# One transformer block on one core: k and v of every batch loaded as nine-token runs and multiplied in four quarters of the array, more transposes done by transfers, a new hand-written order

## The chip, the cores and the metric

The kernel runs on one core of a Trainium2 chip. The metric is device time in microseconds (us), the median of several executions; lower is better. The core has five engines with a queue each: TensorE (PE in the profile, with its weight loads as PEld), VectorE (DVE), ScalarE (ACT), GpSimd (POOL) and SyncE (SP). SP and POOL issue the transfers, and 16 DMA engines carry them out.

## What is computed

Eight batches, eight heads, 576 tokens, 64 channels a head. Linear attention without a softmax, normalised per token and head, is followed by a phase-mixing layer over tokens and a channel layer:

```python
kv  = einsum('bhsd,bhse->bhde', k, v)
out = einsum('bhsd,bhde->bhse', q, kv)
x   = out / sqrt(mean(out*out, -1) + 1e-6) * g_norm      # then heads side by side: (8, 576, 512)
theta = x @ w_theta
y   = w_tok_r @ (x*cos(theta)) + w_tok_i @ (x*sin(theta))  # over the 576 tokens
u   = x + y
result = u + maximum(u @ w_ch, 0)                          # float32, (8, 576, 512)
```

## The kernel before

**Tiling.** A batch is worked on in five token tiles: four full ones of 128 tokens (j = 0 to 3) and one with the last 64 tokens, folded so that two halves of the 512 channels lie side by side. The steps of a batch are: `kv` (PE, fp32, L285; batch 0 L278), copies of kv into the block-diagonal weights `kbd` (ACT L307, DVE L309), q turned so that channels lie on partitions (batches 0 and 1 by PE transposes L302, later ones by SP transfers L330), `raw` = q times kv (PE L344, L353), squares (ACT L366), sums (DVE L375), the power -1/2 on POOL (`rt`, L382; batch 0 by ACT L387 and DVE L392), `x` (DVE L405, L414), x turned into `xT` and scaled (PE transposes named `xps`, L302, then ACT L257 or DVE L259), `th` = theta (PE L464, L467), the argument reduction (ACT L480, DVE L486, L494), sine and cosine (ACT L502, L509), `zm`, `zt` (DVE L531, L520; POOL moves of the tail L537), `y` over tokens (PE L554), `u` in `wn` (DVE L569), u turned back (PE `ups`, L302, L581), `v` (PE L464, L467), the end (DVE L617, L612) and the stores (SP L625, L629).

**Loads of k and v.** For batch 0, `pairs_in` (L191) puts two heads on 128 partitions, each partition holding nine consecutive tokens, 2304 B in one piece; it is called three times for k and three times for v. For the other batches `heads_in` (L199) fetches the first 512 tokens with four tokens a partition, 1024 B in one piece, 1024 pieces a load, and `tails_in` (L205) the last 64 tokens in 512 pieces of 256 B. The half of the tile that the tail leaves empty is set to zero by `pad` (L246).

**kv on the array.** Each fp32 product is two matmul records. In batches 1 to 7 (L285) two heads go together: both contract over 128 partitions, one writes PSUM partitions 0 to 63, the other 64 to 127; four pairs of heads by five tiles by two heads by two records make 80 records. In batch 0 (L278) the two heads of a pair lie on partitions 0 to 63 and 64 to 127, and write the PSUM half of the same number: nine tokens by two heads by two records, 36 for each of four pairs. One PSUM bank of the pool `acc` (four banks, shared by kv, th, y and v) holds a batch's kv.

**Transposes by transfer.** `x_turn_dma` (L425 on) turns x on the SP queue for batches from XD = 5 on, `u_turn_dma` (L594 on) turns u for the batches in UD = (5, 6); in the other batches PE does it through PSUM.

**Order.** Every step is a task; `TURNS` (L29) is one long list of task numbers, and `play` (L84) issues the tasks in just that order, so each engine's queue is fixed by hand. A letter behind a number puts a copy on ACT or DVE; `r15` stands for 15 filler matmuls (`idle`, L649). An engine runs its queue strictly in turn, so a row that waits holds all behind it.

Of the kernel before, what the change touches and what calls it, by code (L numbers as in the profile page):

```python
# [9 lines left out]
FP32 = mybir.dt.float32  # L10
# [19 lines left out]
0 1 8 4 5 6 7 2 18 3 9 10 11 14 15 r15 31 39 32 47 13 16 17 24 25 33 40 34A 48 23 19 20 35 49 41 36  # L30
55 50 42 51 37 52 38A 12 56D 53 54 21 63 71 57 64D 43 72 58 73 65 74 44 r2 137 133 59 45 75 46 60 66
76 138A 134A 61 62 67 77 68 79 89 125 90D 69 70 126 80 91 107 92 108 81D 78 93 98 82 116 117D 94 99
83 95 118 100 129 127 84 85 119 96 86 101 128 87 130 102 120 97 121 88 109 139 141 171 159 122 110
104 123 140 142A 103 124 111 112 105 28 29 26 22 206 27 207 208 30 201 163 135 131 202 113 136 114
106 132D 115 203 204 155 172 160 161 229 173 164 165 156 215 216 162 174 230 166 167 157 147 148 143
168 169 144 158 170 222 145 185 209 210 211 212 149 151 213 186 223D 214 146 150 152 217 231 236 153
243 218 232 237 244 219 154 220 233 205 388 366 377 187 190 175 234 357 188 221 177 192 224 191 176
178 235 225 250 226 251D 238 259 358 227 239 260D 240 193 353 354 514 355 194 356 189 195 252 180
261 196 253 181 262 228 254 245 360 361 241 255 242 263 264 268 362 363 246 256 257 265 266 364 365
247 269D 258 248 359 249 270 286 277 389 271 390 287D 278 288 182 267 391 272 273 183 279 315 367  # L40
289 274 392 275 290 393 291 276 378 311 280 292 293 281 282 379 283 323 312 319 320 430 316 324 284
368 431 294 501 525 502 536 503 504 179 285 369 317 313 318 314 380 505 370 381 321 307 308 325 303
322 326 371 304 305 309 299 300 432 310 382 403 394 433 306 404D 395D 342 301 372 383 396 373 384
397 302 374 434 435 405 347 197 508 509 510 511 406 348 436 437 385 398 407 399 408 438 198 375 386
441 440 439 506 442 295 296 344 400 343 401 513 512 409 376 387 345 402 412 515 526 297 421 422D 298
413 516 410 414 337 423 332 339 349 517 411 415 338 527 416 417 350 528 418 424 419 507 518 529 653
519 425 426 340 530 656 657 658 659 451 542 520 427 428 660 521 420 661D 522 334 537 459 452 662 523
429 543 538 333 335 524 460 453 471 472 473 551 454 539 540 531 461 455 532 552 474 673 684 346 649
650 184 651 652 533 541 456 467 457 468 469 663 534 462 458 535 470 578 327 553 664 328 554 665 579D
463 674 464 560 666 654 465 580 675 555 561D 466 676 556 557 581 558 667 582 677 562 544 563 583 564  # L50
565 685 447 448 329 490 569 545 584 686 566 567 570 585 491 443 449 444 445 546 559 678 687 450 586
446 330 688 571 690 492 668 689 547 691 572 548 669 341 821 810 336 475 679 477 726 573 568 574 727D
670 493 655 589 590 587 588 801 671 797 331 798 832 799 800 494 804 476 575 680 478 681 699 805 806
807 497 728 495 700 549 809 550 808D 496 576 729 682 701 485 692 498 672 730 577 731 480 599 600 591
811 592 593 702 481 486 683 703 822 717 607 601 812 693 705 704 694 594 602 813 814 732 733 823 696
608 603 609 604 605 595 718D 610 734 815 606 824 719 596 597 708 619 735 825 738 802 720 709 706 598
721 695 707 620 615 616 710 621 611 833 826 711 834 697 612 613 623 617 622 722 835 618 836 736 803
737 837 712 698 713 614 625 628 487 816 827 482 714 624 828 817 715 488 626 829 818 483 716 950 629
723 724 838 479 956 872 943 951 952 953 643 767 819 725 847 644 955 820 954D 763 751 764 752 768 769
765 747 748 830 749 638 957 753 831 766 770 873D 754 750 958 839 959 962 848 630 755 960 484 967 855  # L60
489 627 978 944 849 963 756 757 874 850 851 964 631 840 945 946 875 852 639 841 758 961 876 965 947
739 743 740 744 741 968 745 759 842 877 966 742 856 969 853 878 746 970 864D 879 760 640 973 771 761
# [3 lines left out]
898 899 985 904 908 983 896 993D 977 986 889 890 1096 987 900 988 1097 994 891 885 1098 892 909 1107  # L66
1099 995 1108 1018 1001 632 989 996 1109 1110 786 886 913 887 914 888 1100 997 990 1019 998 991 999
1002 1010D 782 915 910 911 1101 1020 783 916 912 1111 992 352 775 1117 637 199 1003 1118 793 937
1102 1021 1022 1023 784 1011 1004 1024 1103 1005 794 499 780 642 1123 917 796 785 648 1104 1025 1012
1119 918 928 923 1026 1013 1120 1006 1014 1105 1007 787 919 1008 924 929 1000 1132D 788 1015 1030  # L70
# [4 lines left out]
1141D 1139 1150 1142 940 1161 1162 935 1151 1152 1074 1163 1143 1164 1084 1144 1085 1069 1075 1146  # L75
# [27 lines left out]
def kernel(  # L103
# [12 lines left out]
    nc = tc.nc  # L116
    B, H, S, D = q.shape
    C = H * D
    P = 128
# [21 lines left out]
    NX, NXE = 7, 4  # L141
    QD = 2

    XD = 5
    UD = (5, 6)

    ZD = 2
# [750 lines left out]
```

## Time and profile before

| | |
|---|---|
| median of 3 runs | 220.95 us (219.73 to 222.49) |
| the profiled execution | 222.68 us, span 220.9 us |
| mean granted TensorE clock in it | 0.973 |
| DMA packets | 70059, of them 39570 under 512 B |
| bytes | 33.06 MB read from HBM, 9.44 MB written |

The profiled execution is 1.73 us above the median, and its time lies 1.8 us above its span. The busy times of an engine are sums over very different stages, so the table of stretches in the prediction is the one to read: a start that waits for loads, a middle in which several engines take turns, and a long last part.

### The profile page before, as it was taken

The page shows a single profiled execution, that of the slowest core. Times are in us where ns is not written, and L with a number is a line of the kernel's source. Part 1 is how long each engine was busy: PE and PEld are TensorE (multiplying, and loading weights), DVE is VectorE, ACT ScalarE, POOL GpSimd, SP SyncE. Part 2 cuts the span into 40 slices and gives each one's busy share as a digit, 9 for nine tenths or more (in the row PEclk, how much of TensorE's full clock was granted, in tenths as well). Part 3 has the DMA queues.
Part 4 walks back from the last instruction along what each step waited for, and adds up shares of the span by engine and source line. Part 5 has one row for each costly group of instructions (what it writes and reads, how often), then busy time and mean ns, then how long its engine had stood idle before and what let it go on. Part 6 is the DMA issues. An engine that isn't in the chain of part 4 may idle for free.

```text
span 220.9 us, 5506 instructions
## 1 busy us (share of the span) xinstructions
PE 200.5 (91%) x2177; PEld 137.7 (62%) x2177; DVE 175.2 (79%) x371; ACT 132.2 (60%) x268; POOL 97.3 (44%) x102
## 2 busy tenths in 40 slices
PE   7398699799799999989999999999999999999991
PEld 2275356596465768757578776866587746756850
DVE  4018649627989989897999988999997999999662
ACT  2028479317499249762788854947865888557050
POOL 8225930002953529556649158435724545204000
PEclk9969769999999999999999999999999999999998
DMA  6999999954999999959999976998980776764374
GB/s 229 274 275 238 236 231 234 271 163 27 260 140 209 297 183 306 122 85 258 307 203 289 137 226 137 240 240 225 163 141 12 225 181 166 178 114 117 110 262 154
DMA packets 70059, 43.43 MB, mean 197 GB/s; under 512 B 39570, under 2 KB 63762, under 8 KB 70034
## 3 DMA queue, kind: packets, MB, share of 16 engines
q1 hardware_dynamic: 55602, 35.73, 64.7%
q0 software_dynamic: 14432, 7.36, 25.0%
q8 instruction: 17, 0.28, 0.5%
q14 instruction: 8, 0.07, 0.1%
HBM read 33.06 MB, written 9.44 MB: 192 GB/s over the span
## 4 chain that ended last, share of the span: by engine, by line
PE 60%; DVE 14%; DMA 9%; POOL 8%; ACT 5%; issue 2%; POOLq 0%; DVEq 0%; ACTq 0%
PE y L554 26%; PE v L464 10%; PE th L464 10%; DMA wth<-in_moe_w_theta_dram 9%; POOL rt L382 5%; PE kv L285 5%; DVE arg L486 2%; DVE ss L375 2%; PE ups L302 2%; PE raw L344 2%; DVE x L405 2%; DVE zm L531 2%; PE th L467 2%; PE xps L302 1%; PE v L467 1%
## 5 line engine op out<-in xcount | busy, mean ns | idle before, releaser
L382 POOL TENSOR_TENSOR rt<-ss,mhalf 128x8 f32<-128x8 f32 (+1 forms) x35 | 54.9, 1572 | 81.7 <-DVE ss L375 81.5
L554 PE MATMUL y<-wT,zm 128*128 128x256 f16 (+1 forms) x512 | 76.0, 286 | 1.9 <-DVE zm L531 1.0
L554 PEld LDWEIGHTS <-zm 128*128 128x128 f16 x512 | 47.7, 98 | 17.2 <-DVE zm L531 2.6
L569 DVE SCALAR_TENSOR_TENSOR wn<-y,gcol,xT 128x256 f16<-128x256 f32 (+2 forms) x72 | 32.6, 478 | 8.2 <-PE y L554 7.7
L464 PE MATMUL th<-wth,xT 128*128 128x512 f16 x128 | 34.2, 395 | 2.0 <-DMA wth<-in_moe_w_theta_dram 1.6
L480 ACT ACTIVATE pt<-th 128x512 f32<-128x512 f32 (+1 forms) x40 | 21.8, 550 | 20.7 <-PE th L464 13.1
L464 PE MATMUL v<-wch,wn 128*128 128x512 f16 x128 | 31.6, 379 | 0.0
L486 DVE SCALAR_TENSOR_TENSOR arg<-pt,th 128x512 f32<-128x512 f32 (+1 forms) x40 | 24.8, 627 | 4.2 <-ACT pt L480 4.0
L509 ACT ACTIVATE sc<-arg,quarter 128x512 f16<-128x512 f32 (+1 forms) x40 | 27.0, 675 | 1.2 <-DVE arg L494 1.1
L502 ACT ACTIVATE sc<-arg 128x512 f16<-128x512 f32 (+1 forms) x40 | 23.4, 587 | 6.9 <-DVE arg L486 6.6
L366 ACT ACTIVATE sqb<-raw 128x512 f32<-128x512 f32 x32 | 18.5, 592 | 14.7 <-PE raw L344 13.4
L405 DVE TENSOR_TENSOR x<-raw,rt 128x512 f16<-128x512 f32 x32 | 21.8, 684 | 3.0 <-POOL rt L382 2.6
L375 DVE TENSOR_REDUCE ss<-sqb 128x8 f32<-128x520 f32 x32 | 21.8, 686 | 2.5 <-ACT sqb L366 2.3
L531 DVE TENSOR_TENSOR zm<-x,sc 128x1024 f16<-128x1024 f16 x32 | 21.7, 682 | 0.5 <-ACT sc L509 0.5
L617 DVE SCALAR_TENSOR_TENSOR us<-v,us 128x512 f32<-128x512 f32 (+1 forms) x32 | 19.4, 616 | 2.0 <-PE v L467 0.8
L307 ACT CAST kbd<-kv 64x256 f16<-64x256 f32 (+1 forms) x28 | 9.4, 334 | 19.1 <-PE kv L278 12.4
L464 PEld LDWEIGHTS <-xT 128*128 128x128 f16 x128 | 11.6, 100 | 13.4 <-issue 3.3
L588 ACT ACTIVATE us<-ups 128x512 f32<-128x512 f16 (+1 forms) x32 | 17.0, 541 | 4.1 <-PE ups L302 2.6
L537 POOL DMA_DIRECT2D zt<-zf x24 | 13.6, 574 | 12.4 <-PE v L467 11.1
L464 PEld LDWEIGHTS <-wn 128*128 128x128 f16 x128 | 11.8, 98 | 11.2 <-issue 0.6
L285 PE MATMUL kv<-vt,kt 128*64 128x64 f32 x560 | 18.3, 223 | 0.0
L554 PE MATMUL y<-wT,zt 128*128 128x320 f16 (+1 forms) x64 | 18.3, 286 | 0.0
(78 smaller groups left out, 249.2 us busy)
## 6 DMA issues: line engine op xcount, KB each, us to landing
kt<-in_k_dram SPq DMA_DIRECT2D x7, 1024.0 KB, 9.1
vt<-in_v_dram SPq DMA_DIRECT2D x7, 1024.0 KB, 8.0
out_dram<-us SPq DMA_DIRECT2D x24, 256.0 KB, 3.4
qh<-in_q_dram POOLq DMA_DIRECT2D x7, 512.0 KB, 11.3
out_dram<-vs SPq DMA_DIRECT2D x8, 256.0 KB, 2.3
zm<-in_moe_w_ch_dram SPq DMA_DIRECT2D x1, 1024.0 KB, 12.0
out_dram<-us SPq DMA_DIRECT2D x16, 64.0 KB, 2.1
kt<-in_k_dram SPq DMA_DIRECT2D x7, 128.0 KB, 7.4
```

What stands on the lines that cost most here:

```text
L285: nc.tensor.matmul(t[i * D:(i + 1) * D, hp - lo, :], kt[b % NKV][:, 2 * hp + i, j, :], vt[b % NKV][:, 2 * hp + i, j, :], start=(j == 0), s ...
L375: nc.vector.reduce_sum(out=ss[:], in_=sq_sb.pop((b, j))[:], axis=AXX)
L382: nc.gpsimd.tensor_tensor(out=rt[:], in0=ss[:], in1=mhalf[:, 0:h], op=ALU.pow)
L405: nc.vector.tensor_tensor(out=x_pair[b, p][:, :, a * HC:(a + 1) * HC].rearrange("p t (h e) -> p h t e", e=D), in0=r[:].rearrange("p (h t e ...
L464: nc.tensor.matmul(t[:], lhs(kc), w[:, kc, :], start=first, stop=last)
L480: nc.scalar.activation(out=pt[:], in_=th_ps[b, j][:], func=AFT.Copy, bias=MAGIC)
L486: nc.vector.scalar_tensor_tensor(out=arg[:, 0, :], in0=pt_sb.pop((b, j))[:], scalar=MAGIC, in1=th_ps.pop((b, j))[:], op0=ALU.subtract, op1 ...
L502: nc.scalar.activation(out=sc[:, 0, :], in_=arg_sb[b, j][:, 0, :], func=AFT.Sin, bias=0.0, scale=-TURN * SHRINK,)
L509: nc.scalar.activation(out=sc_sb[b, j][:, 1, :], in_=arg_sb.pop((b, j))[:, 1, :], func=AFT.Sin, bias=quarter[:], scale=-TURN * SHRINK,)
L531: nc.vector.tensor_tensor(out=dst, in0=x.unsqueeze(1).broadcast_to((P, 2, w)), in1=sc[:], op=ALU.mult)
L554: nc.tensor.matmul(t[:, 0:hi - lo], s, wT[:, w, lo:hi], start=n == 0, stop=n == len(z) - 1)
L569: nc.vector.scalar_tensor_tensor(out=dst, in0=y_in, scalar=gcol[:, 0:1], in1=x_in, op0=ALU.mult, op1=ALU.add,)
```

## The change

1. **Loads.** All batches load k and v with `pairs_in`: one transfer of 512 pieces of 2304 B for k and one for v, where there were four transfers of together 3072 pieces. `heads_in`, `tails_in` and `pad` are gone. Batch 0 comes in two parts instead of three.
2. **kv.** `kv_quad` works on four heads at a time. Each contracts over 64 partitions (r = 0, 1) and writes one half of the PSUM partitions (c = 0, 1), so the four products of a token lie in four different 64x64 quarters of the array. The two row halves write different PSUM banks, so a batch takes two `acc` banks. A batch has 9 tokens x 8 heads x 2 records = 144 records. `kv_out` copies each bank in halves: eight copies of 64x128 a batch where there were four of 64x256 (batch 0: sixteen of 64x64 where there were eight of 64x128).
3. **Transfers for transposes.** XD goes from 5 to 3 and UD from (5, 6) to (4, 5, 6): the x of batches 3 and 4 and the u of batch 4 are turned on the SP queue, which is ten more transfers (four of 128x8x128, two of 128x2x128, four of 128x4x128), and 36 + 16 PE transposes fewer.
4. **Order.** `TURNS` is written anew. There are 20 filler matmuls instead of 17. Of the nine copies of the token weights `wT`, six lie on DVE and three on ACT; before it was the other way round.

```diff
-0 1 8 4 5 6 7 2 18 3 9 10 11 14 15 r15 31 39 32 47 13 16 17 24 25 33 40 34A 48 23 19 20 35 49 41 36
+0 1 7 8 9 10 13 14 12 15 16 20 r11 27 5 6 3 4 19 2 r4 45 37 30D 31 28D 29 46A 38A 17 18 47 r2 53 61
...
-    XD = 5
-    UD = (5, 6)
+    XD = 3
+    UD = (4, 5, 6)
...
-    kt = [const.tile([P, H, NT, D], FP32, name=f"kt{i}") for i in range(NKV)]
+    kt = [const.tile([P, NHP, S], FP32, name=f"kt{i}") for i in range(NKV)]
...
+    def kv_quad(b, g, banks):
+        if banks is None:
+            banks = [ps.tile([P, NG, D], FP32, tag="acc", bufs=4, name="kv") for r in range(2)]
+        for j in range(NN):
+            js = slice(j * D, (j + 1) * D)
+            for c in range(2):
+                for r in range(2):
+                    at = slice(r * D, (r + 1) * D)
                     nc.tensor.matmul(
+                        banks[r][c * D:(c + 1) * D, g, :], kt[b % NKV][at, 2 * g + c, js],
+                        vt[b % NKV][at, 2 * g + c, js], start=(j == 0), stop=(j == NN - 1),
                     )
...
+    def kv_out(b, gs, r, i, eng):
+        at = slice(i * D, (i + 1) * D)
+        lo, n = gs[0], len(gs)
+        for c in range(2):
+            src = kv_ps[b, lo, r][c * D:(c + 1) * D, lo:lo + n, :]
+            h = 2 * c + r
+            dst = kbd[b % 2][at, :, at].rearrange("p (g k) e -> p g k e", k=4)[:, lo:lo + n, h, :]
+            copy_out(eng, dst, src)
...
-        pads = [add("pad", "POOL", lambda: pad(nc.gpsimd, 0), old)] if b == NKV else []
-        k_ = [add(f"load k{b}", "SP", lambda: heads_in(nc.sync, kt[b % NKV], k, b, all8), old),
-              add(f"load k{b}e", "SP", lambda: tails_in(nc.sync, kt[b % NKV], k, b, all8), old),
-              add(f"load v{b}", "SP", lambda: heads_in(nc.sync, vt[b % NKV], v, b, all8), old),
-              add(f"load v{b}e", "SP", lambda: tails_in(nc.sync, vt[b % NKV], v, b, all8), old)]
+        k_ = [add(f"load k{b}n", "SP", lambda: pairs_in(nc.sync, kt[b % NKV], k, b, 0, NHP), old),
+              add(f"load v{b}n", "SP", lambda: pairs_in(nc.sync, vt[b % NKV], v, b, 0, NHP), old)]
...
-        pad(nc.vector, 1)
```

What the new list does is seen at three places. In the rows below a name is the tile written, then what it is made of; a number is the buffer.

The first place is the start of the SP queue. Before, k and v of batch 0 come in six loads, then a tiny transfer (`gate_s`) that waits until the first v is there, the channel weights (`zm_77<-in_moe_w_ch_dram`), and then batch 1 in pieces of four tokens:

```order
L193 DMA kt_64<-in_k_dram 128x576
L193 DMA vt_66<-in_v_dram 128x576
L238 DMA gcol<-in_g_norm_dram 64x1
L244 DMA gate_s<-vt_66 1x1
L235 DMA zm_77<-in_moe_w_ch_dram 128x4x512
L200 DMA kt_65<-in_k_dram 128x8x256
L206 DMA kt_65<-in_k_dram 64x8x64
L200 DMA vt_67<-in_v_dram 128x8x256
L206 DMA vt_67<-in_v_dram 64x8x64
```

Now:

```order
L190 DMA kt_64<-in_k_dram 128x2x576
L190 DMA vt_66<-in_v_dram 128x2x576
L223 DMA gcol<-in_g_norm_dram 64x1 x2
L220 DMA zm_77<-in_moe_w_ch_dram 128x4x512
L229 DMA gate_s<-vt_66 1x1
L190 DMA kt_65<-in_k_dram 128x4x576
L190 DMA vt_67<-in_v_dram 128x4x576
L190 DMA kt_64<-in_k_dram 128x4x576
```

The channel weights have moved ahead of the waiting transfer, and batch 1 is two loads instead of four. The POOL queue beside it begins as before (q of batch 0, `w_tok_i`, `w_theta`, `w_tok_r`).

The second place is the DVE queue where batch 0 ends and batch 1 begins. `wn_85` is u of batch 0, `kbd_75` the kv weights of batch 1, `ss` the sums of batch 1. Before:

```order
L569 SCALAR_TENSOR_TENSOR wn_85<-y,gcol,xT_82 128x320
L309 COPY qT<-qps 128x512
L309 CAST kbd_75<-kv 64x4x64 x2
L569 SCALAR_TENSOR_TENSOR wn_85<-y,gcol,xT_82 128x256 x2
L375 TENSOR_REDUCE ss<-sqb_96 128x8
L569 SCALAR_TENSOR_TENSOR wn_85<-y,gcol,xT_82 128x256
```

Now:

```order
L548 SCALAR_TENSOR_TENSOR wn_85<-y,gcol,xT_82 128x320 x4
L288 CAST kbd_75<-kv 64x2x64 x2
L288 COPY qT<-qps 128x256
L288 CAST kbd_75<-kv 64x2x64 x2
L288 COPY qT<-qps 128x512
L354 TENSOR_REDUCE ss<-sqb_96 128x8
L288 COPY qT<-qps 128x512
L548 SCALAR_TENSOR_TENSOR wn_85<-y,gcol,xT_82 128x256
```

The kv copies and the first sums of batch 1 now stand ahead of the last three rows of u of batch 0. On PE the kv of batch 1 correspondingly stands after 15 of the 24 parts of y of batch 0 (a part is three matmuls), where it stood after 20.

The third place is the POOL queue of batch 1: `rt` are the powers, the DMA rows the loads of a later q. Before:

```order
L382 TENSOR_TENSOR rt<-ss,mhalf 128x8 x2
L212 DMA qh_68<-in_q_dram 128x8x256
L218 DMA qe_71<-in_q_dram 64x4x64
L382 TENSOR_TENSOR rt<-ss,mhalf 128x8 x2
L382 TENSOR_TENSOR rt<-ss,mhalf 128x4
```

Now:

```order
L197 DMA qh_68<-in_q_dram 128x8x256
L203 DMA qe_71<-in_q_dram 64x4x64 x2
L240 TENSOR_SCALAR wch<-zm_77 128x512
L361 TENSOR_TENSOR rt<-ss,mhalf 128x8 x4
L361 TENSOR_TENSOR rt<-ss,mhalf 128x4
```

The load of q that stood between the powers of batch 1 has moved ahead of all of them.

More of the change, by code (lines that the diff above doesn't have):

```diff
@@ L35 @@
[L35 to L39, printed above, removed]
@@ L155 @@
     HALVES = ((0, 2 * P), (2 * P, S))
[L156 to L157 removed]
+    kt = [const.tile([P, NHP, S], FP32, name=f"kt{i}") for i in range(NKV)]
+    vt = [const.tile([P, NHP, S], FP32, name=f"vt{i}") for i in range(NKV)]
     qh = [const.tile([P, H, NJ * D], FP16, name=f"qh{i}") for i in range(NB)]
@@ L717 @@
         ko = {}
[L718 to L726 removed]
+        first = None
+        for g in range(NG):
+            own = b == 0 or not g
+            t = add(f"kq {b} {g}", "PE",
+                    lambda b=b, g=g: kv_quad(b, g, [kv_ps[b, 0, r] for r in range(2)] if g and b else None),
+                    [*k_got[b, g], None if own else first], [PS_ACC, PS_ACC] if own else [])
+            if own:
+                first = t
+            last["kv", b] = t
+            if b and not g:
+                continue
+            gs = [g] if b == 0 else [0, 1]
+            outs = [add(f"ko{len(gs)} {b} {g}{r}{i}", "DVE" if i else "ACT",
+                        lambda e, b=b, gs=gs, r=r, i=i: kv_out(b, gs, r, i, e),
+                        [t, *of("raw", b - 2)], alt=("ACT", "DVE")) for r in range(2) for i in range(2)]
             first.readers = outs
[L728 to L730 removed]
+            ko.update({x: outs for x in gs})
         ko[2] = ko[0] + ko[1]
```

135 lines of the change are left out of this document (35 added, 100 removed), and 37 rows, old and new, of the table TURNS.

## The prediction

> **What bounds the kernel now.** I read the page's first table, then the busy times by stretch, then the chain of waits in order of time, then the groups and the timeline of the engines that the chain names.
>
> ```profile
> PE 200.5 (91%) x2177; PEld 137.7 (62%) x2177; DVE 175.2 (79%) x371; ACT 132.2 (60%) x268; POOL 97.3 (44%) x102
> ```
>
> ```profile
> core 0: us, PE busy (x) PEld busy (x) DVE busy (x) ACT busy (x) POOL busy (x), PEclk, DMA share, GB/s
> 27.80:40.60 12.80, 11.01 (x81) 6.76 (x80) 8.84 (x20) 11.23 (x21) 1.48 (x3) 0.85 1.29 238
> 40.60:52.00 11.40, 10.75 (x157) 8.70 (x155) 4.87 (x10) 2.40 (x5) 0.00 (x0) 1.00 0.68 165
> 52.00:110.00 58.00, 53.63 (x660) 36.94 (x657) 52.73 (x106) 38.15 (x78) 34.27 (x29) 1.00 1.04 207
> 110.00:210.00 100.00, 99.96 (x1015) 69.73 (x1009) 92.56 (x196) 67.38 (x134) 45.09 (x46) 1.00 0.80 173
> 210.00:221.00 11.00, 6.09 (x50) 3.27 (x48) 4.55 (x9) 3.15 (x6) 0.00 (x0) 0.93 0.58 203
> ```
>
> ```profile
> 5.42 20.46 DMA wth<-in_moe_w_theta_dram
> 25.92 1.86 PE th L464 x4
> ...
> 47.56 2.51 PE kv L285 x80
> ...
> 51.80 0.36 PE raw L344 x3
> ...
> 55.31 1.64 POOL rt L382
> 56.95 0.93 POOL qh L212
> 57.88 0.65 POOL qe L218
> 58.53 3.50 POOL rt L382 x2
> ...
> 125.68 2.86 PE y L554 x24
> ```
>
> The reader is to see four stages. Until 25.92 us the chain is one transfer, `w_theta`, and the first th. From 27.8 to 40.6 us ACT is the fullest engine (11.23 of 12.8 us). From 40.6 to 52 us PE works on y alone while DVE and ACT mostly stand (4.87 and 2.40 of 11.4 us), since the norm of batch 1 waits for its kv; then the chain runs through raw, three powers and a load issue on POOL. From 52 to 110 us PE and DVE are both about 92% busy, and PE is without work for 58.00 - 53.63 = 4.4 us. From 110 to 210 us PE has no gap at all: there, and only there, a microsecond of PE work removed is a microsecond of time, as long as DVE (92.6%) keeps up. The tail of 11 us is the same work in both kernels.
>
> **The change, part by part.**
>
> ```profile
> 16.46 1.26 PE L278 MATMUL kv<-vt,kt 64*64 64x64 f32 x36
> ...
> 133.52 0.32 PE L353 MATMUL raw<-kbd,qD 128*64 128x64 f16 x8
> ...
> 138.62 2.55 PE L285 MATMUL kv<-vt,kt 128*64 128x64 f32 x80
> 141.00 0.28 PE L581 MATMUL ups<-ident,wn 128*64 128x128 f16 x4
> ...
> 145.31 0.39 PE L302 MATMUL ups<-ident,wn 128*128 128x128 f16 x4
> 145.53 0.39 PE L344 MATMUL raw<-kbd,qD 128*128 128x128 f16 x4
> ```
>
> ```profile
> L285 PE MATMUL kv<-vt,kt 128*64 128x64 f32 x560 | 18.3, 223 | 0.0
> ...
> L353 PE MATMUL raw<-kbd,qD 128*64 128x64 f16 x48 | 1.9, 200 | 0.1
> ```
>
> *PE transposes.* Four cost 145.53 - 145.31 = 0.22 us, 0.055 each. Fifty-two go (36 of x, 16 of u), all in batches 3 and 4, by the order from the kv of batch 4 on and most of them in the stretch in which PE has no gap: -2.9 us.
>
> *kv in quarters.* A batch costs 141.00 - 138.62 = 2.38 us for 80 records. A record lasts 0.22 us and they start every (2.55 - 0.22)/79 = 0.030 us; batch 0, whose two heads use two of the four quarters, keeps the same pace (36 records in 1.26 us). So two run side by side, and a round of two takes 0.059 us. The new batch has 144 records. If four run side by side at the pace of two, it takes 36 rounds, 2.1 us: -0.24 us a batch, -1.7 us in batches 1 to 7. If still only two do, it takes 72 rounds, 4.25 us: +1.9 us a batch, +13 us in all. No row shows four at once. I take the first end: the quarters that differ in their column half already overlap (L285), quarters that differ in both do too (L278), and the four read the same partitions in the same number of streams as L285; all that is new is two row halves that write one PSUM half, into different banks. In batch 0 the 2.4 us so saved lie in the wait for loads and are worth nothing.
>
> A page speaks against this. The Trainium skill, TensorE: Matmul & The Clock Gate, Part 1, states that start-to-start never falls below about 25 ns however small a matmul is. By that rule 144 records would take 3.6 us, +1.2 a batch, +8.5 us over seven batches. The trace does not agree with it for matmuls that lie in different column halves: the eight of L353 last 0.20 us each and end within 0.32 us, so they start (0.32 - 0.20)/7 = 0.017 us apart.
>
> *Loads at the start.*
>
> ```profile
> q1 hardware_dynamic: 314, 0.65, 65.1%
> ...
> q0 software_dynamic: 981, 1.61, 78.8%
> ...
> q0 software_dynamic: 637, 0.81, 75.4%
> q1 hardware_dynamic: 633, 0.65, 38.6%
> ...
> q1 hardware_dynamic: 1625, 0.40, 111.8%
> ```
>
> ```profile
> 28.32 1.26 ACT L257 ACTIVATE xT<-xps,gcol 128x512 f16<-128x512 f16 x2
> ```
>
> ```profile
> L307 ACT COPY wT<-wps 128x576 f16<-128x576 f16 x6 | 3.6, 634 | 0.2 <-PE wps L643 0.2
> ```
>
> The queue rows are of 6 to 9, 15 to 26, 18 to 24 (two) and 54 to 57 us. From 18 to 24 us SP's queue (q1) and POOL's (q0) move 633 and 637 packets: they take turns one for one. SP's packets are of 1024 B then, and take 38.6% of 16 x 6 us over 633, 58 ns each; the 2304 B packets of 6 to 9 us take 65.1% of 16 x 3 us over 314, 99 ns. In the new kernel the packets of 2304 B also stand beside `w_theta`, which is behind some 900 of the 981 POOL packets that go from 15 to 26 us: 900 x 41 ns / 16 = 2.3 us later, so it lands at about 28 us. What hides this is ACT: by the new order the two scalings of x at 28.32 us (1.26 us) come before the landing, and two of the four copies of `wT` in that stretch (0.6 us each) go to DVE, which has 4 us free there. ACT's 11.23 us shrink by 2.5 to 8.8. It starts 2.3 us later and is through at the same 40.6 us. I cost the start at nothing; without that cover it is +2.3 us. That the channel weights pass the waiting `gate_s` changes nothing, as they stay behind the loads of batch 0 on their queue.
>
> *Loads later.* A load of 1024 + 512 pieces takes (1024 x 58 + 512 x 33)/16 = 4.8 us of the 16 engines (256 B: 111.8% of 16 x 3 us over 1625 is 33 ns), one of 512 x 99 ns takes 3.2. Fourteen loads save 22 us; four big x transposes at 1024 x 33/16 = 2.1, two small at 0.5 and four of u at 1.06 add 13.7. The transfer engines have more room than before, and no load on the chain after 30 us gets later.
>
> *Batch 1 earlier.* Its raw now stands behind 18 parts of y instead of 23 (kv after 15, three more before raw). A part is 3 x 2.86/24 = 0.36 us, so raw comes 5 x 0.36 + 0.24 + 0.22 (a transpose group that follows now) = 2.3 us earlier, into the stretch where ACT and DVE stand. On POOL the load issues between the powers (0.93 + 0.65 us) are ahead of them: the last x of batch 1 comes some 3.8 us earlier. What that is worth is bounded by the 4.4 us that PE waits from 52 to 110 us; below, nothing, if DVE is the limit there. I take half: -2.2 us.
>
> *Copies, scalings, waits.*
>
> ```profile
> L307 ACT CAST kbd<-kv 64x256 f16<-64x256 f32 x20 | 7.3, 364 | 6.5 <-PE kv L285 6.3
> L257 ACT ACTIVATE xT<-xps,gcol 128x512 f16<-128x512 f16 x10 | 6.7, 685 | 0.8 <-PE xps L302 0.8
> L257 ACT ACTIVATE xT<-xd,gcol 128x512 f16<-128x512 f16 x7 | 5.0, 721 | 2.8 <-DMA xd<-x 2.8
> L259 DVE TENSOR_SCALAR xT<-xps,gcol 128x512 f16<-128x512 f16 x10 | 4.6, 474 | 0.1
> L309 DVE CAST kbd<-kv 64x256 f16<-64x256 f32 x8 | 3.4, 421 | 3.6 <-ACT kbd L307 3.4
> L259 DVE TENSOR_SCALAR xT<-xd,gcol 128x512 f16<-128x512 f16 x5 | 1.7, 343 | 0.0
> L307 ACT CAST kbd<-kv 64x128 f16<-64x128 f32 x8 | 2.1, 259 | 12.5 <-PE kv L278 12.4
> ```
>
> ```profile
> xd<-x SPq DMA_TRANSPOSE x9, 3.2
> ```
>
> In batches 1 to 7 the kv copies become 18 on DVE and 38 on ACT. DVE pays 18 x 0.30 (421 less the 29% that halving the width saves on ACT, an estimate) - 8 x 0.42 = +2.0 us, ACT 38 x 0.259 - 20 x 0.364 = +2.6. Scalings: DVE -3 x 0.474 + 0.343 = -1.1, ACT 7 x 0.721 - 5 x 0.685 = +1.6 (the small ones add 1.5). So DVE stays where it is within a microsecond, and with some 3.5 us less PE work from 110 to 210 us it must run at 92.6/96.5 = 96%. That will not be free; nor will the second `acc` bank, which leaves two of four for th, y and v until the last of eight copies (four on an engine, 4 x 0.26, is 1.0 us). Behind a late copy stand raw and, through ACT's own queue, the next pt. No row prices it: between 0 and the whole 3.5 us, I take +1.5, nearer to the lower end because ACT has 33 of 100 us free. A turned x arrives 3.2 us after its issue where PE took 0.22 us plus a queue, but batches 5 to 7 already run so without a gap on PE; on SP it holds only stores and later loads. I cost that at nothing; if the x of a batch is late, th of that batch is late next.
>
> Sum: -2.9 - 1.7 - 2.2 + 1.5 = -5.3 us against the profiled 222.68, that is 217.4. That execution is 1.73 above the median of the three runs, so against the median of 220.95 the forecast is **215.6 us**. About 2%, 4.4 us, is what a measurement of this kernel can tell from no change; the line lies at 216.5.
>
> **The rivals.**
>
> *A. The gain is kept in full.* All of PE's 4.4 us go and nothing is given back: -2.9 - 1.7 - 4.4 = -9, 212. For it: 6.5 us of DVE's standing from 40.6 to 52 us is put to use. Against: DVE at 96% in a strict queue.
>
> *B. DVE or the `acc` banks give it back.* PE shows short waits behind copies or DVE rows after 110 us and batch 1's lead is lost there: -2.9 - 1.7 + 3.5 and nothing for batch 1, 220 (218 to 221).
>
> *C. The quarters run only two at a time.* Each kv takes 4.25 us: 215.6 + 1.7 + 13 = 230, slower. Against: the overlaps named above. It decides on the time of 144 records: from 2.9 us a batch on nothing is gained (217.3 + 7 x 0.52 = 220.95), from 3.5 us on it is slower by 2%.
>
> *D. PE cannot take records up fast enough.* Four at a time means 144 starts in 2.1 us, 0.015 us apart, closer than any row shows. If the pace that PE keeps up lies midway between L353's 0.017 and L285's 0.030, 0.0235 us, a kv takes 3.4 us, +1.0 a batch: 215.6 + 1.7 + 7 = 224.4. For it: no row is as dense for as long. Against: at L353's own pace it would be 2.45 us, +0.07 a batch. The Trainium skill's rule quoted above (TensorE: Matmul & The Clock Gate, Part 1) would put it at 225.8.
>
> *E. The change does not do what it says:* the transposes are replaced but wait on SP behind stores, th is late by what PE saved, 221.
>
> **How the numbers follow.** The forecast (213 to 218.5) has a chance of 0.55, of which 0.38 lies under 216.5 and 0.17 above; A 0.12; B 0.18; C 0.07; D 0.05; E 0.03. Faster by over 2%: 0.38 + 0.12 = 0.50. Within 2%: 0.17 + 0.18 + 0.03 = 0.38. Slower: 0.12. The range takes in the forecast, A and B, 0.85 of the chance: 211 to 221.5, its upper end being E's.
>
> **What would show it.** Right: kv of a batch as 144 records in about 2.2 us; `xps` and `ups` gone from batches 3 and 4; `w_theta` landing near 28 us and the last cosine of batch 0 still near 40.6; raw of batch 1 near 49 us; PE without gaps already from about 50 us on and DVE at 95% or more from 110 to 210. Wrong: a kv of 3.5 us or more (C, D); th waiting for `xd`; PE idle behind `kbd` copies, pt or DVE after 110 us (B); a last cosine of batch 0 after 42 us, which would mean that ACT does not cover the late weights.

## The result, and the profile after

The changed kernel takes 234.04 us (median of 4 runs, 233.03 to 236.67), the kernel before 221.5 us beside it (4 runs, 219.73 to 222.49): the ratio is 1.056, with a 95% interval from 1.0463 to 1.0658. It is slower by 12.5 us, where the forecast was 5.4 us faster; the time lies far above the range. The profiled execution is one of 233.03 us, with a span of 231.3 us.

The first table of the kernel after:

```profile
PE 199.8 (86%) x2576; PEld 131.8 (57%) x2576; DVE 177.9 (77%) x391; ACT 136.1 (59%) x286; POOL 94.9 (41%) x100
```

PE has as much work as before (199.8 us against 200.5) and a span that is 10.4 us longer, so nearly all of the loss is PE standing. The busy time by stretch says where (the columns are those of the prediction's table):

```profile
27.80:40.60 12.80, 11.30 (x80) 6.69 (x78) 10.46 (x24) 9.41 (x18) 5.21 (x5) 0.79 1.19 277
40.60:52.00 11.40, 10.00 (x211) 7.67 (x209) 7.31 (x18) 3.29 (x9) 2.58 (x2) 1.00 0.89 109
52.00:110.00 58.00, 50.87 (x819) 35.77 (x817) 47.55 (x99) 36.56 (x80) 29.11 (x26) 0.97 0.97 184
110.00:210.00 100.00, 93.96 (x1124) 61.15 (x1122) 90.17 (x195) 73.03 (x150) 44.04 (x42) 1.00 0.89 187
```

From 52 to 110 us PE stands for 7.1 us (4.4 before), from 110 to 210 us for 6.0 us, where it had stood for 0.04. DVE went down with it, from 92.6 to 90.2 us: it is not the new bound. What PE waits for, with the time in all, the number of waits and the longest:

```profile
PE kv L261 <- issue: 6.5, 4, 4.0
PE th L443 <- ACT xT L238: 1.8, 4, 0.5
PE y L533 <- issue: 1.3, 1, 1.3
PE kv L261 <- DMA vt<-in_v_dram: 1.2, 1, 1.2
PE th L443 <- DVE xT L240: 1.1, 2, 0.7
```

"issue" is time in which the engine waited for nothing that the profile shows. PE had no such wait in the kernel before; here it is 7.8 us. Of that 6.5 us stand inside the new product, and one wait of 1.3 us a few rows behind that of batch 6. PE's timeline for batches 2, 3 and 4:

```profile
61.10 2.20 PE L261 MATMUL kv<-vt,kt 64*64 64x64 f32 x132
65.06 0.45 PE L261 MATMUL kv<-vt,kt 64*64 64x64 f32 x12 [1.77 <-issue]
...
84.11 2.33 PE L261 MATMUL kv<-vt,kt 64*64 64x64 f32 x144
...
93.82 2.19 PE L261 MATMUL kv<-vt,kt 64*64 64x64 f32 x131
99.98 0.45 PE L261 MATMUL kv<-vt,kt 64*64 64x64 f32 x13 [3.96 <-issue]
```

Batch 3 runs as forecast, 144 records in 2.33 us: four quarters do overlap, at (2.33 - 0.22)/143 = 0.0148 us a record, 59 ns for a round of four. Batches 2 and 4 run at the same pace and then stop, 132 and 131 records in, for 1.77 and 3.96 us, and go on. All their data had landed: the stop is no wait on a semaphore.

One row of the DMA queues gives the first hint at what the stop is. The page of the kernel after lists a queue that carries instructions, which is of no size among the others:

```profile
q8 instruction: 20, 0.33, 0.6%
```

Twenty packets of 0.33/20 MB = 16 KB. PE has 2 x 2576 = 5152 matmuls and weight loads, 258 for each packet (the kernel before has 17 packets for 4354, 256 each). So PE's program seems to come to it in blocks of some 256 instructions, and a product in quarters, 144 pairs, is longer than one block.

### The profile page after: what moved, and what is told of

Its sections match the earlier page's. It is cut to its first block, busy times and chain, and to the rows that moved or that the text cites. A ratio compares the mean times of both kernels' runs of the same rounds, so it can differ in the third digit from the quotient of the medians.

```text
span 231.3 us, 6328 instructions
## 1 busy us (share of the span) xinstructions
PE 199.8 (86%) x2576; PEld 131.8 (57%) x2576; DVE 177.9 (77%) x391; ACT 136.1 (59%) x286; POOL 94.9 (41%) x100
## 4 chain that ended last, share of the span: by engine, by line
PE 39%; DMA 24%; DVE 17%; ACT 8%; issue 7%; POOL 2%; SPq 1%; DVEq 0%; POOLq 0%; ACTq 0%
PE y L533 18%; DMA xd<-x 10%; DMA wnt<-in_moe_w_tok_i_dram 9%; PE v L443 6%; PE th L443 5%; DVE arg L465 4%; DMA ud<-wn 4%; PE kv L261 3%; DVE zm L510 3%; DVE arg L473 2%; DVE wn L548 2%; PE raw L323 2%; ACT kbd L286 2%; ACT xT L238 2%; ACT sc L488 1%
## 5 line engine op out<-in xcount | busy, mean ns | idle before, releaser
L361 POOL TENSOR_TENSOR rt<-ss,mhalf 128x8 f32<-128x8 f32 (+1 forms) x35 | 53.8, 1540 | 79.0 <-DVE ss L354 78.8
L533 PE MATMUL y<-wT,zm 128*128 128x256 f16 (+1 forms) x512 | 77.9, 289 | 2.9 <-issue 1.3
L533 PEld LDWEIGHTS <-zm 128*128 128x128 f16 x512 | 48.2, 99 | 21.1 <-DVE zm L510 3.6
L443 PE MATMUL th<-wth,xT 128*128 128x512 f16 x128 | 33.0, 389 | 2.9 <-ACT xT L238 1.8
L261 PE MATMUL kv<-vt,kt 64*64 64x64 f32 x1152 | 20.6, 224 | 7.7 <-issue 6.5
L481 ACT ACTIVATE sc<-arg 128x512 f16<-128x512 f32 (+1 forms) x40 | 22.8, 584 | 4.9 <-DVE arg L465 4.7
L261 PEld LDWEIGHTS kv<-vt,kt 64*64 64x64 f32 x1152 | 18.9, 138 | 11.3 <-issue 9.3
L567 ACT ACTIVATE us<-ups 128x512 f32<-128x512 f16 (+1 forms) x28 | 14.4, 533 | 12.3 <-PE ups L281 11.4
L286 ACT CAST kbd<-kv 64x128 f16<-64x128 f32 (+1 forms) x44 | 11.1, 252 | 16.6 <-PE kv L261 15.1
L516 POOL DMA_DIRECT2D zt<-zf x24 | 13.1, 550 | 13.7 <-PE v L443 11.7
## 6 DMA issues: line engine op xcount, KB each, us to landing
vt<-in_v_dram SPq DMA_DIRECT2D x7, 1152.0 KB, 10.4
zm<-in_moe_w_ch_dram SPq DMA_DIRECT2D x1, 1024.0 KB, 12.3
```

What stands on the lines that cost most here:

```text
L261: nc.tensor.matmul(banks[r][c * D:(c + 1) * D, g, :], kt[b % NKV][at, 2 * g + c, js], vt[b % NKV][at, 2 * g + c, js], start=(j == 0), stop ...
L361: nc.gpsimd.tensor_tensor(out=rt[:], in0=ss[:], in1=mhalf[:, 0:h], op=ALU.pow)
L443: nc.tensor.matmul(t[:], lhs(kc), w[:, kc, :], start=first, stop=last)
L481: nc.scalar.activation(out=sc[:, 0, :], in_=arg_sb[b, j][:, 0, :], func=AFT.Sin, bias=0.0, scale=-TURN * SHRINK,)
L533: nc.tensor.matmul(t[:, 0:hi - lo], s, wT[:, w, lo:hi], start=n == 0, stop=n == len(z) - 1)
```

## The experiments

Four theories were set against each other. *Theory 1*: PE runs out of instructions inside the quartered product. *Theory 2*: x and u, turned by transfers, come late (transfers of x make up 10% of the chain of the kernel after, those of u 4%). *Theory 3*: the new order and its start lose the time. *Theory 4*, formed after the first four runs: the product's second `acc` bank and its eight copies in place of four. All runs in one table, the part that each leaves or changes in a few words, the median, and the ratio to the runs of the kernel before beside it:

| run | kernel | us | ratio, 95% interval |
|---|---|---|---|
| after | the whole change | 234.04 | 1.056, 1.046 to 1.066 |
| e1 | before, with the new loads and product | 234.28 | 1.059, 1.048 to 1.071 |
| e2 | before, with the new transfers | 249.26 | 1.129, 1.122 to 1.136 |
| e3 | after, instructions moved by 90 | 229.82 | 1.040, 1.031 to 1.049 |
| e4 | after, halves of the product apart | 237.36 | 1.076, 1.066 to 1.086 |
| e5 | before, product in two banks, eight copies | 226.62 | 1.019, 1.016 to 1.021 |
| e6 | after, x and u turned back to PE | 242.66 | 1.094, 1.087 to 1.100 |
| e7 | after, with the old loads and product | 226.15 | 1.018, 1.014 to 1.022 |
| e8 | before, one bank, eight copies | 221.98 | 1.005, 1.001 to 1.009 |
| e9 | e1, instructions moved by 90 | 236.30 | 1.070, 1.063 to 1.076 |
| e10 | products alone | 92.74 (one execution) | |
| e11 | e7, loads of v ahead of transfers | 230.52 | 1.040, 1.034 to 1.047 |
| e12 | after, two quarters at a time | 237.95 | 1.076, 1.069 to 1.083 |

**e1, the product and its loads alone, in the order of before.** The code is that of after with the old limits for the transfers; the list of turns is that of before, by the names of the tasks:

```
-    XD = 3
-    UD = (4, 5, 6)
+    XD = 5
+    UD = (5, 6)
 the list of turns: that of before, with
-kv 1 0   kv 1 1   kv 1 2   kv 1 3
+kq 1 0   kq 1 1
```

> This is the kernel before with one part of the change: k and v of all batches in nine-token runs and their product in four quarters; x and u are turned as before (x by transfers from batch 5, u in batches 5 and 6) and the tasks keep the order of before. Theory 1 (PE runs out of instructions inside the quartered product: 288 instructions go by in 2.1 us, while a refill of 256 takes 2.5 us and more): gaps that end on nothing the profile shows stand inside or just behind some of the product's blocks, 0.4 to 4 us each, and eat the 1.7 us that the shorter blocks save; 220 to 226 us, and at least 2 us of PE's idle time at the product is put down to issue. Theory 2 (the turned x and u come late): the transfers that it blames are not in this kernel, so 217 to 221 us. Theory 3 (the new order and its start cost the time): the order is that of before, so 217 to 221 us, and no gaps at the product.

It took 234.28 us: this part alone loses as much as the whole change, more than any theory said. The gaps of theory 1 are there, but they are 3.5 us of 13. PE's waits in it:

```profile
PE kv L261 <- issue: 3.5, 2, 3.0
PE y L533 <- ACT kbd L286: 1.7, 1, 1.7
PE y L533 <- DVE kbd L288: 1.6, 2, 0.8
PE kv L261 <- DVE us L596: 1.0, 3, 0.4
```

Among the rest are new waits for the copies of the product (`kbd`) and, inside the product after its first two records, for a second bank that `fin` (`us`) has yet to free. That is theory 4. With the 4.1 us that e5 finds for it, 7.6 of the 13 us have a name; the other 5 stay open. The new loads go in together with the product here and were not run alone.

**e2, the transfers alone, in the order of before.**

```
-    XD = 5
-    UD = (5, 6)
+    XD = 3
+    UD = (4, 5, 6)
 the list of turns: that of before, each xd and ud right behind the last task that it needs
```

> This is the kernel before with the other part of the change: x by transfers from batch 3 on and u in batches 4 to 6, each put behind the last task that it needs; k, v and their product as before. Theory 1: no block of the product is run in four quarters, so no gaps on issue in it, and 218 to 223 us. Theory 2: th of batches 3 and 4 waits for xd, 1 to 5 us at a time, and finish of batch 4 for ud; 226 to 230 us. Theory 3: 218 to 222 us.

It took 249.26 us, more than theory 2 said. Up to batch 3 it runs as before; then PE waits for what hangs on the transfers:

```profile
PE raw L344 <- DVE x L405: 5.0, 1, 5.0
PE th L467 <- DVE xT L259: 4.7, 2, 4.2
PE th L464 <- DVE xT L259: 4.7, 2, 4.5
PE raw L344 <- DMA qD<-qh: 3.8, 1, 3.8
```

The order of before puts th of these batches close behind x, where a transpose by PE had been quick enough. SP now waits with its queue for x, and the turned q of the next batch (`qD`) stands behind it on that queue. So the transfers need the new order. What they cost within it, e6 and e7 ask.

**e3, the kernel after with its instructions moved.** In the idle work of the first wait, behind 11 wide matmuls, which comes to:

```
+        for _ in range(45):
+            nc.tensor.matmul(t[:, 0:1], ident[:], fill[:, 0:1], start=True, stop=True)
```

> This is the kernel after with 45 more matmuls of one column in PE's wait for the first loads, 90 instructions, which move all that follows against the blocks of 256 in which the instructions come. Theory 1: the gaps inside the product of batches 1, 2 and 4 (0.4, 1.8 and 4.0 us) go, since the refill that they wait for is now asked for some 75 instructions ahead of the block; in batch 6, where the border now falls on the start of the block, a new gap of 1 to 4 us stands in it, and behind those of batches 3 and 5 gaps of up to 1 us may come. Time 227 to 234 us. Theory 2 and theory 3: the gaps are waits for data or for queues, which 90 instructions in a wait at the start do not move: the same gaps at batches 1, 2 and 4, and 233 to 235 us.

229.82 us, 4.2 us less than after (3.5 by the two ratios of the table), for 45 matmuls *more* at a place where PE waits anyway. The gaps at batches 1 and 2 are gone, that of batch 4 is down from 3.96 to 1.80 us, and one of 1.95 us stands some 40 instructions behind the product of batch 3, where the move brought the border of a block:

```profile
88.71 0.40 PE L281 MATMUL xps<-ident,x 128*128 128x128 f16 x4 [1.95 <-issue]
96.81 1.14 PE L261 MATMUL kv<-vt,kt 64*64 64x64 f32 x58 [1.80 <-issue]
```

The gap expected in batch 6 didn't come, and batch 4 kept one, so the places were told only in part. That they go with the position in the program is shown: 7.8 us of gaps became 3.8, and the time fell by as much.

**e4, the two halves of each product three PE tasks apart.** For batch 1, for instance:

```
 kq 1 0
-kq 1 1
 qte 1 4
 qt 1 0
 y0 0 0 0
+kq 1 1
```

> This is the kernel after with the second half of each product, batches 1 to 7, three PE tasks later, so that 144 instructions of it are followed by 2 to 3 us of other work. Theory 1: no gap of over 0.5 us on issue inside the product; 6 us of PE's idle time there go, and 226 to 231 us come of it. Theory 2: the gaps go or stay, but what th waits for is the transfers, so the time stays within 232 to 235 us. Theory 3: no change in the time, 232 to 235 us, or up to 1 us more since the eight heads of the product are copied later.

The gaps went, as theory 1 said (0.6 us are left), and the time rose by 3.3 us, which it had not said. PE now waits for what the later product makes late:

```profile
PE th L443 <- DVE xT L240: 3.6, 2, 2.2
PE th L443 <- ACT xT L238: 2.4, 4, 1.4
PE y L533 <- ACT kbd L286: 1.2, 2, 0.7
PE kv L261 <- issue: 0.6, 1, 0.6
```

So the gaps aren't the whole loss. That a later end of the product costs through the copies, raw, the norm and x is what these waits suggest; it was not run by itself.

**e5, two banks and eight copies in the kernel before**, with its old product; **e8, eight copies and one bank.** They part theory 4 (e5's cut first, then e8's):

```
-        for lo, n in ((0, 2), (2, 2)) if b == 0 else ((0, NHP),):
+        for lo, n in ((0, 2), (2, 2)):
```

```
         for k_ in range(2):
-            copy_out(eng, dst[:, :, k_, :], t[k_ * D:(k_ + 1) * D, :, :])
+            for m in range(0, n, 2):
+                copy_out(eng, dst[:, m:m + 2, k_, :], t[k_ * D:(k_ + 1) * D, m:m + 2, :])
```

> This is the kernel before with one side effect of the change alone: the product of every batch is collected in two acc banks (heads 0 to 3, 4 to 7) and copied out by eight copies of 64x128, where batches 1 to 7 had one bank and four copies of 64x256; loads, instructions of the product and the rest of the order are as before. Theory 4 (what the first part loses beside its refill gaps is the second bank and the doubled copies): 226 to 230 us, with PE's waits for kbd copies and for us, arg and um to free acc banks larger by 4 us or more. Theory 1 (the gaps on instructions are the main cost of the quartered product): 219 to 223 us, and no gaps on issue.

> This is the kernel before with each of the copies of the product out of its one bank cut in two, for batches 1 to 7: eight copies of 64x128 as the change has them, and one bank as before. Two banks and eight copies together had cost 4.1 us. Theory 4a (the copies do it: seven times four more fixed shares of an instruction on ACT and DVE, and the last of them later): 224 to 227 us. Theory 4b (the second acc bank does it, since y, th and v have one bank fewer to go ahead in): 221 to 223 us.

With both, 226.62 us: 1.85% or 4.1 us, at the lower end of what theory 4 said. With the copies alone, 221.98 us: 0.45% or 1.0 us, which is theory 4b. The other 3.1 us are the second bank's, by the difference of the two runs (about 1 us either way by their intervals). In e5 the two banks are filled one after the other, in the change both at once; what they cost there was not run.

**e6, x of batches 3 and 4 and u of batch 4 turned by PE again**, in the order of after, each transpose as close ahead of its scaling as two `tr` banks let it:

```
-    XD = 3
-    UD = (4, 5, 6)
+    XD = 5
+    UD = (5, 6)
```

> This is the kernel after with x of batches 3 and 4 and u of batch 4 turned by PE again, as in the kernel before; loads, the quartered product and otherwise the order are as after. Theory 2 (turned x and u come late): the waits of 3 to 7.5 us for xd and ud go from the chain for batches 3 and 4, and the time falls to 225 to 230 us though PE has 2.2 us more to do. Theories 1 and 4: the transfers are not what costs; 233 to 237 us, and the gaps on issue remain, some 6 us in all, though at other places, since the transposes move the stream by 100 and more instructions.

242.66 us, 8.6 us more than after and above every range. In this order the same transposes on PE lose more than the transfers do. How much of the 8.6 us is due to my places for the transposes is not known, so the run does not clear the transfers.

**e7, the loads and the product of before in the order of after**, the transfers kept:

```
 the list of turns: that of after, with (here batch 1's product and batch 2's loads)
-kq 1 0   kq 1 1   load k2n              load v2n
+kv 1 0   kv 1 1   kv 1 2   kv 1 3   load k2   load k2e   load v2   load v2e
```

> This is the kernel after with the loads and the product of the kernel before in the order of after: k and v by four tokens and tails from batch 1 on, 80 full-height pairs of matmuls in one bank, four copies out. The transfers of x and u and the new order stay. Theories 1 and 4 (the quartered product loses the time): no gaps on issue, fewer waits for copies, 220 to 225 us. Theories 2 and 3 (transfers, order and start lose it): 231 to 237 us.

226.15 us: of the 12.5 us, some 8 go with the loads and the product (7.9 by the times, 8.4 by the ratios), and no wait on issue is left. Theories 1 and 4 hold for that part, and 4 us stay with the order and the transfers, a little more than they allowed. PE's busy time in e7, for the stretches from 40.6 us on:

```profile
40.60:52.00 11.40, 10.69 (x156) 8.44 (x155) 7.09 (x18) 3.93 (x9) 0.00 (x0) 1.00 1.19 216
52.00:110.00 58.00, 56.06 (x687) 39.46 (x685) 54.09 (x110) 41.07 (x84) 33.15 (x28) 1.00 1.13 205
110.00:210.00 100.00, 93.30 (x918) 62.12 (x917) 87.84 (x186) 69.07 (x137) 42.43 (x43) 1.00 0.91 186
210.00:223.00 13.00, 7.87 (x68) 5.04 (x66) 5.42 (x10) 2.55 (x5) 0.00 (x0) 0.98 0.51 170
```

They sum to 167.9 us, against 10.75 + 53.63 + 99.96 + 6.09 = 170.4 before, with 1829 matmuls in place of 1882, which is the 52 transposes and one: 2.5 us of transposes did leave PE. And up to 110 us the new order stands better than the old, 1.9 us of waits in place of 4.4. From 110 us on PE stands for 6.7 us where it had no gap, and these are the largest of its waits there:

```profile
PE kv L285 <- DMA vt<-in_v_dram: 2.0, 1, 2.0
PE th L464 <- ACT xT L257: 1.9, 2, 1.1
PE y L554 <- DMA zt<-zf: 1.2, 2, 0.6
```

**e11, the loads of v of batches 5 to 7 moved up on SP's queue** in e7, to take that 2.0 us away (here batch 5):

```
 load k5e
+load v5   load v5e
 st 0 10
 qde 4 2
 xde 3 4
 xd 3 0
 qd 4 1
 xd 3 2
 st 1 30
-load v5   load v5e
```

> This is the kernel with the old product in the new order, with the loads of v of batches 5 to 7 moved ahead of the transposing transfers on SP's queue, right behind those of k. Theory 2, in the form that is left (more transfers on one queue make what stands behind them late): PE's wait of 2.0 us for v of batch 5 goes, and 223.5 to 225.5 us come of 226.2. If that wait only stood ahead of another one, 226 to 227 us.

It took 230.52 us, 4.4 us *more*, against both expectations. SP's rows of e7 and then of e11 show why (start, time on SP):

```profile
98.72 2.52 SPq L433 DMA_TRANSPOSE xd<-x  x2
...
106.71 0.42 SPq L200 DMA_DIRECT2D vt<-in_v_dram  x1
107.17 0.72 SPq L206 DMA_DIRECT2D vt<-in_v_dram  x1
```

```profile
91.83 2.47 SPq L200 DMA_DIRECT2D vt<-in_v_dram  x1
94.35 4.59 SPq L206 DMA_DIRECT2D vt<-in_v_dram  x1
...
103.81 2.58 SPq L433 DMA_TRANSPOSE xd<-x  x2
```

The same two loads that SP hands out in 0.42 and 0.72 us behind the transfers hold it for 2.47 and 4.59 us when they follow the loads of k at once, and the turned x of batch 3 starts 5.1 us later. The wait for v of batch 5 is gone, but PE now waits for turned x at two th, 3.39 us for batch 3 and 5.17 us for batch 4, which e7 doesn't have.

**e9, e3's 45 matmuls in e1.**

> This is the kernel of the first run (product and loads of the change in the order of before) with 45 matmuls of one column in PE's first wait, 90 instructions. Theory 1: its gaps on issue, 3.0 us in batch 2 and 0.5 us in batch 6, go, since the borders of the instruction blocks now lie some 170 instructions inside these products; one of up to 1.5 us may come at batch 5, whose border moves to 20 instructions behind its start. 229 to 232 us, against 234.3 us. If the gaps are of another kind they stay, and so does the time.

The gaps at batches 2 and 6 are gone and one of 1.27 us stands at batch 5, as expected; but one of 2.30 us in batch 7 and one of 0.99 behind the product of batch 3 are new, 4.6 us in all against 3.5. The time is 236.30 us, 2 us more, which is within the spread of e1's executions (232.23 to 236.06). The gaps follow the position again. That their sum falls was wrong: a move helps one product and harms the next.

**e10, the product by itself**: the list of turns is left out, and in its place stand a warm-up, six products with all queues quiet, and six beside loads.

```
+        for _ in range(6):
+            kv_quad(0, 0, None)
+            kv_quad(0, 1, [kv_ps[0, 0, r] for r in range(2)])
```

> This kernel holds nothing of the computation but products: six of batch 0 one behind the other with all loads landed and the queues quiet, a warm-up ahead of them, then the same six while loads of k and v run. Theory 1: in the quiet part PE stops once in some 256 instructions, 0.3 to 1 us each time, so that a product of 288 instructions takes some 2.6 to 3.4 us on the mean in place of 2.1; beside the loads the stops are longer, 1 to 4 us, and a product takes 3.5 to 6 us. If instructions come fast enough and the gaps of the kernel after are of another kind, the six take 2.1 to 2.2 us each in both parts.

PE's timeline, three rows of the quiet part and three beside the loads:

```profile
29.61 2.10 PE L209 MATMUL kv<-vt,kt 64*64 64x64 f32 x128 [1.63 <-issue]
33.33 2.09 PE L209 MATMUL kv<-vt,kt 64*64 64x64 f32 x128 [1.63 <-issue]
...
40.52 2.10 PE L209 MATMUL kv<-vt,kt 64*64 64x64 f32 x128 [1.36 <-issue]
...
57.90 3.69 PE L209 MATMUL kv<-vt,kt 64*64 64x64 f32 x128 [3.23 <-issue]
63.54 3.69 PE L209 MATMUL kv<-vt,kt 64*64 64x64 f32 x128 [1.96 <-issue]
70.29 3.40 PE L209 MATMUL kv<-vt,kt 64*64 64x64 f32 x128 [3.05 <-issue]
```

This settles what the gaps are. With nothing else on the chip PE stops after exactly 128 matmuls and their 128 weight loads, 256 instructions, in each of the six blocks that follow the first stop: 2.10 us of work, then 1.63 us of standing, once 1.36. By the trace's records of the transfers the next 16 KB start 1.1 to 1.5 us after PE has begun the block ahead of them, take 1.0 to 1.4 us, and PE goes on some 1.4 us after they have landed: 3.73 us a block, 14.6 ns an instruction (once 3.46 us), is the fastest that these runs show the program delivered over several blocks. The seven quiet products (one stands ahead of the six) took 3.85 us each on the mean, not 2.1; the six beside loads 5.4. Theory 1 had the mechanism and set it too low.

The Trainium skill, Runtime: NRT & Kernel Launch, Instruction fetch mechanics, states the block (256 instructions, 16 KiB) and that the next is fetched while the present one is executed, and the runs agree. It also calls the cost mostly hidden; here it is 1.63 us in 3.73.

**e12, the same 288 instructions at half the pace**, so that only two quarters run side by side:

```
-        for j in range(NN):
-            js = slice(j * D, (j + 1) * D)
-            for c in range(2):
+        for c in range(2):
+            for j in range(NN):
+                js = slice(j * D, (j + 1) * D)
                 for r in range(2):
```

> This is the kernel after with the loop over the column halves outside the loop over the tokens, so that only two quarters run side by side: the same 288 instructions of a product, the same banks and copies, at about half the pace, some 4.2 us for a product. Theory 1 (instructions come at 256 in 3.7 us at best, as the bursts showed, 14.6 ns each, so the pace of four quarters is not to be had for a whole product): the gaps on issue in the products all but go, under 1 us in sum against 6.5, and the time is 232 to 238 us, though PE is busy with products for about 2 us more in each batch. If the pace of the four quarters is worth what its records say: 8 times 2 us more on PE, 244 to 250 us.

```profile
L261 PE MATMUL kv<-vt,kt 64*64 64x64 f32 x1152 | 32.8, 224 | 3.6 <-issue 2.4 <-DMA vt<-in_v_dram 1.2
85.48 3.90 PE L261 MATMUL kv<-vt,kt 64*64 64x64 f32 x144
```

The product keeps PE busy for 32.8 us in place of 20.6, 12.2 us more, and the time is 237.95 us, 3.9 more. Its gaps fell from 6.5 to 2.4 us, less than expected. As a whole the run says what the quartered pace is worth: it makes the product 12.2 us shorter on PE, and that saves 3.9 us of time.

## Why the prediction was wrong

*The quarters, -1.7 us.* "If four run side by side at the pace of two, it takes 36 rounds, 2.1 us" holds for a block that runs undisturbed (batch 3). The step that failed is to price it as that pace alone. 288 instructions in 2.1 us are 7.4 ns each, and over several blocks they come at about 14.6 ns (e10). The product of before, 160 instructions in 2.38 us, took 14.9 ns each, about what delivery allows, and its trace has no stop that would point to a limit. In batches 1 to 7 the rows of the new product sum to 17.5 us, against 18.3 before, and 6.5 us of stops stand inside it: in place of -1.7 us the term came to roughly +5.7. Whether a product stops depends on where in the program its block borders fall and on how full the DMA queues are: none in batch 3, 3.96 us in batch 4, where the packet of instructions stood among data. By the trace's records it started 3.8 us after PE had begun the block ahead, against 1.1 to 1.5 us on the quiet chip. In the stretch around it, from 96 to 100 us of after, the data queues held more than the 16 engines' whole time:

```profile
q1 hardware_dynamic: 496, 1.10, 83.2%
q0 software_dynamic: 447, 0.14, 30.8%
q8 instruction: 1, 0.02, 1.6%
```

Of the rivals, D ("PE cannot take records up fast enough", 224.4; its terms sum to 224.3) had the right place and sign and the wrong mechanism: the starts can be as close as needed. Rival C's pace, 4.25 us a batch, is nearly what the program sustains, though not because only two quarters run. B (the banks) and E (transposes on SP) each named another part of the loss and made it too small.

*Copies and banks, +1.5 us.* The mechanism was named ("nor will the second `acc` bank, which leaves two of four for th, y and v"), the size was not: 4.1 us in the order of before, of which the copies, which I had priced row by row, are 1.0, and the bank, which no row priced, 3.1.

*The transposes, -2.9 us.* 2.5 us did leave PE. The step that failed is "I cost that at nothing": behind 110 us PE stands for 6.7 us in e7, most of it for v, turned x and `zt`. That batches 5 to 7 ran so before without a gap was no evidence for batches 3 and 4, whose x stands on SP's queue among loads and stores that were elsewhere before. e11 shows how tight that queue is. How much of the 6.7 us is the transfers' and how much the order's is not known.

*Batch 1 earlier, -2.2 us, and the start, 0.* These go together. The first th and the first raw of batch 1 in after, then the kv of batch 2 in before (that of after is shown with the result):

```profile
30.96 2.96 PE L443 MATMUL th<-wth,xT 128*128 128x512 f16 x8
...
51.46 0.39 PE L323 MATMUL raw<-kbd,qT 128*128 128x128 f16 x4
```

```profile
61.16 1.36 PE L285 MATMUL kv<-vt,kt 128*64 128x64 f32 x40
```

The first th comes 5.0 us later, not 2.3: `w_theta` landed 25.2 us after its issue at 5.4, at 30.6 us where 28 was forecast, and the chain of after up to then is another transfer, the tail of `w_tok_i` at 24.9 us, with the transposes of these weights and of x behind it. ACT's cover held roughly: the last cosine of batch 0 ends at 41.7 us, 1.1 later than before. But raw of batch 1 is at 51.5 us where "near 49" was forecast, and the kv of batch 2 starts at 61.1 us, as it did before (61.2). So the start, priced at nothing, seems to have taken what the order gave to batch 1 (no run undoes the start alone), and the -2.2 us did not come.

*DVE at 96%.* It did not come to that: 90.2 us from 110 to 210 us.

*The sum that the runs give.* 4.0 us for order, start and transfers (e7), 4.1 for the second bank and the copies (e5), 4.2 that moving the instructions gives back (e3; 3.5 by the ratios): 12.3 of 12.5, or 11.6. That it closes so well is partly luck. The terms come from different orders, e3 still holds 3.8 us of gaps, the same move in e1 gained nothing, and the same terms leave 5 of e1's 13 us open. Shown are the stops for instructions, the cost of the second bank in the order of before, and a remainder of 4 us that stays without the new product, each in rough size. Open is how that remainder divides between the transfers and the order, since undoing either alone (e2, e6) breaks the other, and what the new loads cost or save by themselves. None of these kernels is faster than the one before, and none of the runs points to one that would be.

## What to carry to other kernels

Before an engine's work is cut into smaller and faster instructions, count them: here PE was never fed faster over several blocks than 256 instructions in some 3.7 us, so 288 small matmuls and weight loads are worth about 4.2 us unless slower work stands around them, whatever their own pace. A resource that no row prices (a second bank, a place in another engine's queue) should get its price from a run, or a wide range; here these were two of the three parts of the loss. And a busy share of 100% in one stretch doesn't make each microsecond there a gain: in e7 2.5 us of work left PE, and it stood for 6.7 us in the stretch that had no gap.

## What was not expected of the hardware

- PE's program comes in blocks of 256 instructions, and each packet starts 1.1 to 1.5 us after PE begins the block ahead: 3.73 us a block on a quiet chip, and PE stops for 1.63 us of it when it is through in 2.10. Beside loads it stops for 2.0 to 3.2 us. Moving all instructions by 90 changed the time of the same work by 4.2 us (e3).
- Four quarters of 64x64 run side by side: 59 ns for a round of four, 14.8 ns from start to start.
- A long stop costs twice. Behind that of 3.96 us PE's granted clock was 0.67 for 4 us and 0.90 for the next 4 (rows below, from after), an estimated 0.33 x 4 + 0.10 x 4 = 1.7 us more; behind those of 1.77 us and, in e1, 2.99 us it stayed at 1.00. In e10 the block behind the stop of 3.23 us ran at 0.50 (3.69 us in place of 2.10), and that behind the stop of 3.05 us at 0.56 (3.40 us). Two shorter stops can do the same: 2.30 and 1.72 us with 0.34 us of work between them, in e9, were followed by 0.50. The Trainium skill, TensorE: Matmul & The Clock Gate, HAM oscillation, warns of idle gaps over about 3.4 us; the runs agree roughly, with the border for a single stop between 2.99 and 3.05 us.

```profile
100.00:104.00 4.00, 4.00 (x38) 2.59 (x39) 1.00 (x3) 2.43 (x8) 1.01 (x1) 0.67 1.45 174
104.00:108.00 4.00, 4.00 (x38) 3.46 (x37) 2.91 (x6) 1.68 (x3) 1.55 (x1) 0.90 0.08 12
```

- Handing out a load is not free for the queue's engine: the same 64x8x64 piece held SP for 0.72 us in e7 and for 4.59 us in e11, right behind three other loads.
